# RWKV-7 attention and a cosine router: chunks of 64 steps instead of 32, two heads on the two row halves of TensorE

## The chip, the cores and the metric

The kernel runs on one core of a Trainium2 chip. The time is the device time of one execution in microseconds; the median of several runs counts. TensorE multiplies, VectorE, ScalarE and GpSimd work element by element, and SyncE (SP) issues most of the DMA transfers.

## What is computed

The first part is a recurrence over 768 steps for 4 batch elements and 8 heads, with a 40x40 state for each. Its output, as rows of 320 features for 3072 tokens, goes through a router with 8 experts, of which each token takes one; the expert is two matrix products with a ReLU between them.

```python
for t in range(S):
    y[:, :, t] = np.einsum('bhd,bhde->bhe', rt, state)
    Sa = np.einsum('bhde,bhe->bhd', state, at)
    state_decay = state * wt[:, :, None, :] - np.einsum('bhd,bhe->bhde', Sa, bt)
    state = state_decay + np.einsum('bhd,bhe->bhde', vt, kt)
...
logits = xn @ en.T / tau
expert_idx = np.argmax(logits, axis=1)
...
    h = np.maximum(x[mask] @ w1[e], 0.0)
    out[mask] = gate_w[mask, None] * (h @ w2[e])
```

## The kernel before

All arithmetic is in float32. The steps are cut into tiles of 128 (6 for each of 4 batch elements, 24 in all, `groups`), and a tile into 4 chunks of 32 steps. Features (40) or steps (128) stand on the partitions. Each tile goes through two generators.

`prepare` does what doesn't need the state: two scans over the decay w (L202, L205), scaling of a, k and b, transposes of the scaled inputs (`ln`, `an`, `kn`, `bn`, L237), four products between all 128 steps and all 128 steps of a tile for each head (`between`, L248: `ne`, `ge`, `fe`, and later `he`), of which a mask keeps the four 32x32 blocks on the diagonal (L251). Then it inverts the 32x32 triangular blocks in five levels: the first from a mask alone, then four times `w_ps` (L300), a copy on ScalarE, `x_ps` (L310), a predicated copy on VectorE (L314). These products are 32x32, and the four chunks stand on the diagonal of the array. Last come `te` (the inverse spread out to 128x128), `gv` and `pt`.

`advance` takes the state through the four chunks: `u_ps` (L359) against the state, `s_ps` (L367, L372) for the next state, `sn` (the state transposed, L384), `y_ps` against it (L388). At the end of a tile come `ut`, `he`, the rest of y, and the router: `xr`, its transposes `xt_ps`, the logits `lg_ps` (L418), some fifteen small steps on VectorE and ScalarE, and the store to `x_rows`.

While `advance` runs on a tile, two steps of `prepare` of the next are taken for each of its own, and a scheduler puts the instructions of every engine into one order from the dependencies and its own estimates. The buffers set when loads can start: most inputs have one buffer, some two. The eight parts of the expert weights `w2` are loaded one after the other in the attention (`load_w2`, L91, on ScalarE's queue) into memory of their own. `w1` is loaded when the attention has ended (L472 on SP, L475 on ScalarE), into memory that the attention used.

The experts run in 31 blocks of 128 tokens: gather, transposes (L607), `h_ps` (L628), transposes (L645), `y_ps` (L655), scatter. Which expert a block takes is a number in a register, and `h_ps` and `y_ps` index the whole of w1 and w2 with it, so the first `h_ps` waits for all of w1 and the first `y_ps` for all of w2.

A product in float32 is two instructions (passes) on TensorE, each with a load of its weights and a matmul; a transpose is one. In the trace, "xN" counts these.

Of the kernel before, what the change touches and what calls it, by code (L numbers as in the profile page):

```python
# [9 lines left out]
FP32 = mybir.dt.float32  # L10
BF16 = mybir.dt.bfloat16
I32 = mybir.dt.int32
# [8 lines left out]
L = 32  # L21
NCK = P // L

# [6 lines left out]
def kernel(  # L30
# [26 lines left out]

    nc = tc.nc
# [7 lines left out]
    CH = H * NCK  # L66
# [3 lines left out]
    XBUF = 3  # L70

# [6 lines left out]
    w2_sb = persist.tile([P, E, FC, DM], FP32, name="w2_sb")  # L78
    w2f = w2_sb.rearrange("p e c d -> p (e c d)")
# [10 lines left out]
    def load_w2(e):  # L90
        nc.scalar.dma_start(  # L91
            out=w2_sb[:, e], in_=moe_w2[e].rearrange("(c p) d -> p c d", p=P)
        )

    with ExitStack() as attn:
# [3 lines left out]
        mmp = attn.enter_context(tc.tile_pool(name="mmp", bufs=5, space=PSUM))  # L99
# [6 lines left out]
        blk = cst.tile([P, P], FP32, name="blk")  # L106
        nc.vector.memset(blk, 0.0)
        for c in range(NCK):
            nc.vector.memset(blk[L * c : L * c + L, L * c : L * c + L], 1.0)
        upper = cst.tile([P, P], FP32, name="upper")  # L110
        nc.gpsimd.affine_select(
            out=upper, in_=blk, compare_op=ALU.is_gt, fill=0.0, base=0,
            pattern=[[1, P]], channel_multiplier=-1,
        )
        nlower = cst.tile([P, P], FP32, name="nlower")
        nc.gpsimd.affine_select(
            out=nlower, in_=blk, compare_op=ALU.is_gt, fill=0.0, base=0,
            pattern=[[-1, P]], channel_multiplier=1,
        )
        nc.vector.tensor_scalar(nlower, nlower, -1.0, None, ALU.mult)  # L120
        icomp = cst.tile([P, L], FP32, name="icomp")
        nc.vector.tensor_reduce(
            icomp.unsqueeze(2), ident.rearrange("p (c j) -> p j c", c=NCK), axis=AX.X, op=ALU.add
        )
        rowi = cst.tile([P, L], I32, name="rowi")
        coli = cst.tile([P, L], I32, name="coli")
        nc.gpsimd.iota(rowi, pattern=[[0, L]], base=0, channel_multiplier=1)
        nc.gpsimd.iota(coli, pattern=[[1, L]], base=0, channel_multiplier=0)
        nc.vector.tensor_scalar(rowi, rowi, L - 1, None, ALU.bitwise_and)
        rowf = cst.tile([P, L], FP32, name="rowf")  # L130
        colf = cst.tile([P, L], FP32, name="colf")
# [5 lines left out]
        for j in range(L.bit_length() - 1):  # L137
            m = cst.tile([P, L], I32, name=f"level{j}")
# [6 lines left out]
        W1C = CH * (L + 1) + 1  # L145
        first = cst.tile([D, W1C], FP32, name="first")
        nc.vector.memset(first, 0.0)
        nc.vector.memset(first[:, 0 :: L + 1], 1.0)
        decay = cst.tile([D, W1C], FP32, name="decay")
        nc.vector.memset(decay[:, 0 :: L + 1], 0.0)  # L150


        emb = two.tile([P, XW], FP32, tag="xr", name="emb")[0:E, 0:DM]
# [3 lines left out]
        emb2 = two.tile([P, XW], FP32, tag="xr", name="emb2")[0:E, 0:DM]  # L157
# [13 lines left out]
        def h3(t):  # L171
            return t[:, 0:DM].rearrange("p (h d) -> p h d", h=H)

        def half(t):
            return t.rearrange("p (h x) -> p h x", h=4)

        state = {}
        groups = [(b, i) for i in range(NT) for b in range(B)]
        loaded = {}

        def load(g):
            b, i = groups[g]
            d = {}
            for nm, src in (("w", wT), ("a", aT), ("k", kT), ("b", bT), ("v", vT), ("r", rT)):
                t = (two if nm == "r" else one).tile([D, H, P], FP32, tag=f"in_{nm}", name=f"in_{nm}")
                nc.sync.dma_start(out=t, in_=src[b, i])
                d[nm] = t
            d["vn"] = two.tile([P, H, D], FP32, tag="vn", name="vn")
            nc.sync.dma_start(out=d["vn"], in_=v[b, i])
            loaded[g] = d  # L190

        def prepare(g, d):

            d.update(loaded.pop(g))
            ck = "p (x t) -> p x t"


            body = decay[:, 0 : W1C - 1].rearrange(ck, t=L + 1)
            nc.scalar.copy(body[:, :, 1:], d["w"].rearrange("p h (c t) -> p (h c) t", t=L))
            lam = one.tile([D, W1C], FP32, tag="lam", name="lam")  # L200
            suf = one.tile([D, W1C], FP32, tag="suf", name="suf")
            nc.vector.tensor_tensor_scan(  # L202
                lam, decay, first, initial=0.0, op0=ALU.mult, op1=ALU.add
            )
            nc.vector.tensor_tensor_scan(  # L205
                suf[:, ::-1], decay[:, ::-1], first[:, ::-1], initial=0.0, op0=ALU.mult, op1=ALU.add
            )
            lam3 = lam[:, 0 : W1C - 1].rearrange(ck, t=L + 1)
            lam_l = two.tile([D, CH], FP32, tag="lam_l", name="lam_l")
            nc.vector.tensor_copy(lam_l, lam3[:, :, L])  # L210
            d["lamL"] = lam_l.rearrange("p (h c) -> p h c", c=NCK)
            inv_l = two.tile([D, CH], FP32, tag="inv_l", name="inv_l")
            nc.vector.reciprocal(inv_l, lam_l)
            inv = d["w"].rearrange("p h (c t) -> p (h c) t", t=L)
            nc.gpsimd.tensor_tensor(
                inv,
                suf[:, 1:].rearrange(ck, t=L + 1)[:, :, 1:],
                bc(inv_l, [D, CH, L], 2),
                ALU.mult,
            )  # L220

            def chunked(t):
                return t.rearrange("p h (c t) -> p (h c) t", t=L)

            lx = one.tile([D, W1C], FP32, tag="suf", name="lx")[:, 0 : H * P].rearrange(
                "p (h t) -> p h t", h=H
            )
            nc.scalar.copy(chunked(lx), lam3[:, :, 0:L])
            nc.vector.tensor_tensor(d["a"], d["a"], lx, ALU.mult)
            nc.gpsimd.tensor_tensor(d["k"], d["k"], d["w"], ALU.mult)  # L230
            nc.gpsimd.tensor_tensor(d["b"], d["b"], d["w"], ALU.mult)


            for nm, src in (("ln", lx), ("an", d["a"]), ("kn", d["k"]), ("bn", d["b"])):
                ps = h3(bank(f"{nm}_ps"))
                for h in range(H):
                    nc.tensor.transpose(ps[:, h], src[:, h], ident[0:D, 0:D])  # L237
                d[nm] = (one if nm == "an" else two).tile([P, H, D], FP32, tag=nm, name=nm)
                nc.scalar.copy(d[nm], ps)
            yield  # L240

            def between(nm, lhs, rhs, mask, pool):
                t = pool.tile([P, H, P], FP32, tag=nm, name=nm)
                for q in range(2):
                    ps = half(bank(f"{nm}_ps"))
                    for j in range(4):
                        h = 4 * q + j
                        nc.tensor.matmul(  # L248
# [12 lines left out]
            if g + 1 < NG:  # L261
                load(g + 1)
# [464 lines left out]
```

## Time and profile before

| | us |
|---|---|
| median of 3 runs | 2146.05 (2144.84 to 2147.27) |
| profiled execution | 2144.23 |
| its span, first to last instruction | 2142.5 |
| TensorE busy | 2034.7 |
| VectorE, ScalarE, GpSimd busy | 692.4, 377.9, 298.1 |

In a row of the timeline stand the start, the time from there to the end of the last instruction of the group, the engine, the line, the operation, what it writes and reads (weights and moving operand), shapes, and the count. The difference of two starts is the time that a group holds the engine. The granted clock is a share of 2.4 GHz: 0.50 is the level of 1.2 GHz, 1.00 that of 2.4.

### The profile page before, as it was taken

Reading aid. Unit: us, or ns where it says so; the run is one execution under the profiler, and the core shown is the slowest. Engines: PE = TensorE matmul, PEld = TensorE weight load, DVE = VectorE, ACT = ScalarE, POOL = GpSimd, SP = SyncE. Lnnn points to the kernel's source line nnn. Section 1 sums busy time; section 2 is a strip of 40 time slices with the busy share of each in tenths; the row PEclk is TensorE's granted clock in tenths of the full one; section 3 lists DMA queues with packets and bytes.
Section 4 is the critical chain, followed back from the end, with each engine's and each line's share of the span. In section 5 each row is a group of like instructions: output and inputs, shape, how many; then the busy total and the mean of one; then the engine's idle time right before and its main releaser. Section 6 shows DMA issues by size and latency. Waiting matters only on the chain. (4 is left out here: it accounts for less than half of the span.)

```text
span 2142.5 us, 54098 instructions
## 1 busy us (share of the span) xinstructions
PE 2034.7 (95%) x24944; PEld 1725.1 (81%) x24944; DVE 692.4 (32%) x1374; ACT 377.9 (18%) x769; POOL 298.1 (14%) x240
## 2 busy tenths in 40 slices
PE   4999999999999999999999999999999948999998
PEld 4899989898989898989898988898898843555554
DVE  5332433243324332443234333432443231111111
ACT  1112112211211122112111211121211111111111
POOL 3011101110111011101110111011101011111110
PEclk9655555555555555555555555555555558999999
DMA  8000000000000000000000000000000042000000
GB/s 243 14 26 15 20 20 26 11 21 23 23 14 21 23 25 12 21 24 23 14 21 23 23 15 21 23 23 15 24 23 8 5 140 88 25 27 28 21 17 4
DMA packets 28481, 63.81 MB, mean 30 GB/s; under 512 B 4052, under 2 KB 18398, under 8 KB 28256
## 3 DMA queue, kind: packets, MB, share of 16 engines
q1 hardware_dynamic: 16320, 39.88, 6.3%
q10 hardware_dynamic: 8960, 12.58, 2.0%
q0 software_dynamic: 2976, 7.89, 1.2%
q8 instruction: 198, 3.24, 0.6%
q14 instruction: 27, 0.22, 0.0%
HBM read 53.60 MB, written 9.02 MB: 29 GB/s over the span
## 5 line engine op out<-in xcount | busy, mean ns | idle before, releaser
L628 PE MATMUL h_ps<-w_sb,xT 128*128 x372 | 185.5, 624 | 9.2 <-DMA w_sb<-in_moe_w_dram 9.2
L270 POOL TENSOR_TENSOR te<-xt,blk 128x1024 f32<-128x1024 f32 x24 | 56.4, 2349 | 976.1 <-DVE xt L314 976.1
L628 PEld LDWEIGHTS h_ps<-w_sb,xT 128*128 128x128 f32 x372 | 63.3, 190 | 115.6 <-issue 111.0
L655 PE MATMUL y_ps<-w_sb,hT 128*128 x496 | 138.8, 433 | 0.0
L388 PE MATMUL y_ps<-sn,in_r 40*32 40x40 f32 x1536 | 126.4, 265 | 6.8 <-ACT sn L386 6.8
L367 PE MATMUL s_ps<-vn,kn 32*40 32x40 f32 x1472 | 130.1, 265 | 0.0
L386 ACT COPY sn<-sn_ps 40x320 f32<-40x320 f32 x96 | 40.1, 418 | 506.0 <-PE sn_ps L384 506.0
L372 PE MATMUL s_ps<-un,bn 32*40 32x40 f32 x1472 | 126.1, 263 | 0.4 <-DVE gs L444 0.4
L359 PE MATMUL u_ps<-st,pt 40*32 40x40 f32 x1536 | 125.6, 264 | 0.0
L300 PE MATMUL w_ps<-xt,ne 32*32 32x32 f32 x6144 | 121.1, 238 | 3.9 <-DVE xt L314 3.9
L388 PEld LDWEIGHTS y_ps<-sn,in_r 40*32 40x32 f32 x1536 | 107.3, 162 | 20.9 <-ACT sn L386 10.0
L367 PEld LDWEIGHTS s_ps<-vn,kn 32*40 32x40 f32 x1472 | 108.2, 173 | 15.0 <-issue 5.4
L310 PE MATMUL x_ps<-ws,xn 32*32 32x32 f32 x6144 | 104.0, 237 | 16.5 <-ACT ws L305 12.9
L655 PEld LDWEIGHTS y_ps<-w_sb,hT 128*128 128x128 f32 x496 | 91.7, 190 | 34.2
L359 PEld LDWEIGHTS u_ps<-st,pt 40*32 40x32 f32 x1536 | 106.7, 162 | 14.5 <-issue 8.8
L300 PEld LDWEIGHTS w_ps<-xt,ne 32*32 32x32 f32 x6144 | 99.7, 149 | 18.6 <-DVE xt L314 4.3
L372 PEld LDWEIGHTS s_ps<-un,bn 32*40 32x40 f32 x1472 | 108.6, 174 | 7.4 <-DVE gs L444 0.5
L310 PEld LDWEIGHTS x_ps<-ws,xn 32*32 32x32 f32 x6144 | 90.9, 150 | 25.7 <-ACT ws L305 16.3
L251 DVE TENSOR_TENSOR he<-he_ps,upper 128x512 f32<-128x512 f32 x48 | 32.8, 684 | 230.1 <-PE he_ps L248 230.1
L305 ACT COPY ws<-w_ps 128x256 f32<-128x256 f32 x96 | 35.7, 372 | 362.5 <-PE w_ps L300 362.5
L248 PE MATMUL fe_ps<-in_r,in_v 40*128 40x128 f32 x384 | 98.4, 435 | 0.0
L322 PE MATMUL gv_ps<-vn,ge 128*128 128x40 f32 x384 | 92.3, 416 | 0.0
(179 smaller groups left out, 3172.7 us busy)
## 6 DMA issues: line engine op xcount, KB each, us to landing
w_sb<-in_moe_w_dram ACTq DMA_DIRECT2D x8, 1280.0 KB
w_sb<-in_moe_w_dram SPq DMA_DIRECT2D x8, 1024.0 KB
x_rows<-xr SPq DMA_DIRECT2D x24, 160.5 KB
in_w<-in_wT_dram SPq DMA_DIRECT2D x24, 160.0 KB
in_a<-in_aT_dram SPq DMA_DIRECT2D x24, 160.0 KB
in_k<-in_kT_dram SPq DMA_DIRECT2D x24, 160.0 KB
in_b<-in_bT_dram SPq DMA_DIRECT2D x24, 160.0 KB
in_v<-in_vT_dram SPq DMA_DIRECT2D x24, 160.0 KB
```

The source lines that it names most:

```text
L248: nc.tensor.matmul(ps[:, j], lhsT=lhs[:, h], rhs=rhs[:, h], start=True, stop=True)
L270: nc.gpsimd.tensor_tensor(t.rearrange("p h (c j) -> p h c j", c=NCK), bc(x, [P, H, NCK, L], 2), bc(blk.rearrange("p (c j) -> p c j", c=NCK ...
L300: nc.tensor.matmul(ps[rows, h], lhsT=ne[rows, h, rows], rhs=xt[rows, h], start=True, stop=True, skip_group_check=True,)
L310: nc.tensor.matmul(ps[rows, h], lhsT=xd[rows, h], rhs=ws[rows, h], start=True, stop=True, skip_group_check=True,)
L322: nc.tensor.matmul(gv_ps[:, h], lhsT=ge[:, h], rhs=d["vn"][:, h], start=True, stop=True)
L359: nc.tensor.matmul(u_ps[rows, h], lhsT=d["pt"][:, h, rows], rhs=st[:, h], start=False, stop=True, skip_group_check=True,)
L367: nc.tensor.matmul(s_ps[:, h], lhsT=d["kn"][rows, h], rhs=d["vn"][rows, h], start=(h == 0), stop=False, skip_group_check=True,)
L372: nc.tensor.matmul(s_ps[:, h], lhsT=d["bn"][rows, h], rhs=un[rows, h], start=False, stop=True, skip_group_check=True,)
L386: nc.scalar.copy(sn, sn_ps)
L388: nc.tensor.matmul(y_ps[rows, h], lhsT=d["r"][:, h, rows], rhs=sn[:, h], start=False, stop=False, skip_group_check=True,)
L628: nc.tensor.matmul(ps, lhsT=d["xT"][0:kn, c], rhs=w1f[0:kn, ds(ek * (len(KC) * F) + c * F + q * 512, 512)], start=(c == 0), stop=(c == len ...
L655: nc.tensor.matmul(ps, lhsT=d["hT"][:, c], rhs=w2f[:, ds(d["ek"] * (FC * DM) + c * DM, DM)], start=(c == 0), stop=(c == FC - 1),)
```

## The change

The attention is written anew; the experts are as before but for the loading of their weights.

- Two batch elements go together as one unit (12 units). A chunk is 64 steps long, so a tile has two. Of a pair of heads one has its 40 features on partitions 0 to 39, the other on 64 to 103; the index of such pairs is x (8 in a unit), of the head in a pair par. An input of a unit comes in four loads (w in sixteen); the partitions between are filled once at the start, on GpSimd.
- `gram` replaces `between`: only products within a chunk, 64x64, with par and chunk naming the part of the array. The inverse is still of 32x32 blocks, in four levels after the first (now from `nd`, small products of its own); the lower left 32x32 block of the inverse of a chunk comes from one more step (the half level and `z`).
- Products that write steps are cut into 32 columns of the array (`sub`): `gv`, u against the state (named u_ps at L422 in the order), u, y against `sn`, y, `lg`.
- `pt`, `an` and the product that spreads `te` are gone. `sn` is a product with an identity, no transpose, and the old state comes into `s_ps` by a product with the identity.
- Two steps of `prepare` are still taken for each of `advance`, and `kn`, `ge`, `bn`, `fe` stand between w and x of the four levels (`fill`). More inputs have two or three buffers.
- PSUM has seven rotating banks and one for s, before five and three.
- `w2` gets memory that the attention has used, and is loaded behind it with w1, w1 on SP and w2 on ScalarE.

```diff
-L = 32
+L = 64
+SB = 32
+NP = 4
+OFF = 64
...
-    w2_sb = persist.tile([P, E, FC, DM], FP32, name="w2_sb")
...
+        units = [(i, bp) for i in range(NT) for bp in range(BP)]
+        feat = [slice(0, D), slice(OFF, OFF + D)]
+        chunk = [slice(0, L), slice(L, P)]
+        sub = [slice(SB * q, SB * q + SB) for q in range(P // SB)]
...
+        def gram(nm, lhs, rhs):
+            ps = [bank(f"{nm}_ps").rearrange("p (x t) -> p x t", x=NX) for _ in range(2)]
+            for x in range(NX):
+                for c in range(2):
+                    for par in range(2):
+                        nc.tensor.matmul(
+                            ps[par][chunk[c], x], lhsT=lhs[feat[par], x, chunk[c]],
+                            rhs=rhs[feat[par], x, chunk[c]],
+                            start=True, stop=True, skip_group_check=True,
+                        )
+            return ps
...
+            for m_ in levels[1:]:
+                xd = turned(xt)
+                ps = blocks(
+                    "w_ps", lambda ps, m, q: mm(ps[sub[q], m], ne[sub[q], m, own(q)], xt[sub[q], m])
+                )
+                ws = two.tile([P, NM, SB], FP32, tag="ws", name="ws")
+                nc.scalar.copy(ws, ps)
+                yield
+                if fill:
+                    fill.pop(0)()
+                ps = blocks(
+                    "x_ps", lambda ps, m, q: mm(ps[sub[q], m], xd[sub[q], m], ws[sub[q], m])
+                )
+                nc.vector.copy_predicated(xt, bc(m_, [P, NM, SB], 1), ps)
+                yield
...
+            def with_state(ps, lhs, st, c):
+                for x in range(NX):
+                    for s_ in range(2):
+                        q = 2 * c + s_
+                        for par in range(2):
+                            mm(ps[par][sub[q], x], lhs[feat[par], x, sub[q]], st[feat[par], x, 0:D])
...
+                    for x in range(NX):
+                        for par in range(2):
+                            mm(s_ps[feat[par], x], kn[rows, 2 * x + par], vn[rows, 2 * x + par], False)
...
+                                mm(
+                                    u_ps[bb][sub[2 * c + s_], p, par],
+                                    d["te"][rows, mi(x, par), SB * s_ : SB * s_ + SB],
+                                    ru[rows, x, par],
+                                )
...
-            if g % 2 == 1 and g // 2 < E:
-                load_w2(g // 2)
...
+    w2_sb = wpool.tile([P, E, FC, DM], FP32, name="w2_sb")
...
-        nc.scalar.dma_start(out=w1_sb[0 : KC[2][1], e, 2], in_=moe_w1[e, 2 * P : DM])
+        nc.sync.dma_start(out=w1_sb[0 : KC[2][1], e, 2], in_=moe_w1[e, 2 * P : DM])
+        nc.scalar.dma_start(
+            out=w2_sb[:, e], in_=moe_w2[e].rearrange("(c p) d -> p c d", p=P)
+        )
```

On TensorE, in the middle of a tile, the order of before puts the two products of a level (w_ps, x_ps, for 8 heads) between the state's products for a chunk of 32 steps:

```order
L310 MATMUL x_ps<-ws,xn 32x32 x32
L359 MATMUL u_ps<-st_2247,pt 32x40 x8
L367 MATMUL s_ps<-vn,kn 40x40 x6
L300 MATMUL w_ps<-xt,ne 32x32 x32
L367 MATMUL s_ps<-vn,kn 40x40 x2
L372 MATMUL s_ps<-un,bn 40x40 x4
L310 MATMUL x_ps<-ws,xn 32x32 x32
```

and the changed kernel, at the same place, for 16 heads and a chunk of 64:

```order
L348 MATMUL w_ps<-xt,ne 32x32 x64
L301 MATMUL kn_ps<-ident,in_k_150 128x104 x8
L348 MATMUL x_ps<-ws,xn 32x32 x64
L422 MATMUL s_ps<-un_172,bn 40x40 x16
L492 MATMUL ut_ps<-ident,un_172 104x64 x8
L348 MATMUL w_ps<-xt,ne 32x32 x64
L241 MATMUL ge_ps<-in_a_144,in_k_150 64x64 x32
L348 MATMUL x_ps<-ws,xn 32x32 x64
```

The products that stood behind the levels (kn, ge, bn, fe) now stand between w and x of one level, and the state's products between two levels. On TensorE at the end of a tile and into the next, before:

```order
L331 MATMUL pt_ps<-te,an 40x128 x7
L347 MATMUL y_ps<-kn,fe 128x40 x2
L237 MATMUL ln_ps<-ident,lx 128x40 x8
L237 MATMUL an_ps<-ident,in_a 128x40 x8
L237 MATMUL kn_ps<-ident,in_k 128x40 x8
L237 MATMUL bn_ps<-ident,in_b 128x40 x8
L248 MATMUL ne_ps<-in_b,in_a 128x128 x4
```

and in the changed kernel at the end of a unit:

```order
L422 MATMUL y_ps<-kn,fe 32x40 x64
L422 MATMUL y_ps<-bn,he 32x40 x64
L530 MATMUL xt_ps<-ident,xr 128x128 x2
L530 MATMUL xt_ps<-ident,xr 64x128
L422 MATMUL s_ps<-st_0_176,ident 104x320
L541 MATMUL lg_ps<-embT,xs 32x8 x8
```

There pt, an and the whole-array products are gone, and y is made of 32-column pieces right ahead of the router's transposes.

## Rows read from the trace of the kernel before

**Rows 1.** The page: busy time, share and instructions by engine; granted clock in 40 slices.
```profile
PE 2034.7 (95%) x24944; PEld 1725.1 (81%) x24944; DVE 692.4 (32%) x1374; ACT 377.9 (18%) x769; POOL 298.1 (14%) x240
...
PEclk9655555555555555555555555555555558999999
```

**Rows 2.** TensorE timeline: one place in two tiles, the last tile.
```profile
643.70 1.17 PE L248 MATMUL ne_ps<-in_b,in_a 40*128 40x128 f32 x8
...
1640.72 1.47 PE L248 MATMUL ne_ps<-in_b,in_a 40*128 40x128 f32 x8
...
1706.64 0.25 PE L384 MATMUL sn_ps<-ident,st 40*40 40x40 f32 x2
...
1735.71 1.55 PE L418 MATMUL lg_ps<-embT,xs 128*128 128x8 f32 x6 [0.46 <-ACT xs L414]
```

**Rows 3.** TensorE timeline of the tile from 606 us on: one group of each kind.
```profile
606.10 1.27 PE L359 MATMUL u_ps<-st,pt 40*32 40x40 f32 x16
607.30 0.75 PE L367 MATMUL s_ps<-vn,kn 32*40 32x40 f32 x8
607.98 1.08 PE L310 MATMUL x_ps<-ws,xn 32*32 32x32 f32 x64
...
612.89 0.72 PE L384 MATMUL sn_ps<-ident,st 40*40 40x40 f32 x8
613.54 3.21 PE L322 MATMUL gv_ps<-vn,ge 128*128 128x40 f32 x14
...
618.33 1.91 PE L397 MATMUL ut_ps<-ident,un 128*40 128x128 f32 x8
...
642.70 0.67 PE L237 MATMUL kn_ps<-ident,in_k 40*128 40x40 f32 x8
...
647.07 3.62 PE L248 MATMUL ge_ps<-in_a,in_k 40*128 40x128 f32 x16
```

**Rows 4.** Groups by line and shape: busy us, mean ns, idle before.
```profile
L300 PE MATMUL w_ps<-xt,ne 32*32 32x32 f32 x6144 | 121.1, 238 | 3.9 <-DVE xt L314 3.9
...
L202 DVE TENSOR_TENSOR_SCAN lam<-decay,first 40x1057 f32<-40x1057 f32 x24 | 55.5, 2314 | 6.6 <-ACT decay L199 6.6
...
L305 ACT COPY ws<-w_ps 128x256 f32<-128x256 f32 x96 | 35.7, 372 | 362.5 <-PE w_ps L300 362.5
L229 DVE TENSOR_TENSOR in_a<-in_a,lx 40x1024 f32<-40x1024 f32 x24 | 33.4, 1392 | 3.1 <-ACT lx L228 3.1
...
L251 DVE TENSOR_TENSOR he<-he_ps,upper 128x512 f32<-128x512 f32 x48 | 32.8, 684 | 230.1 <-PE he_ps L248 230.1
```

**Rows 5.** TensorE timeline: first gram, and first transposes of the second tile.
```profile
26.07 3.76 PE L248 MATMUL ne_ps<-in_b,in_a 40*128 40x128 f32 x16
...
69.58 0.69 PE L237 MATMUL ln_ps<-ident,lx 40*128 40x40 f32 x8
```

**Rows 6.** VectorE timeline: a fill at the start.
```profile
1.27 0.94 DVE L147 MEMSET first<- 40x1057 f32 x1 [0.16 <-issue]
```

**Rows 7.** Chain that ended last: start us, us, what.
```profile
1743.00 19.50 DMA w_sb<-in_moe_w_dram
```

**Rows 8.** TensorE timeline: first products of the experts.
```profile
1779.73 8.40 PE L628 MATMUL h_ps<-w_sb,xT 128*128 x12 [9.18 <-DMA w_sb<-in_moe_w_dram]
...
1795.33 0.70 PE L655 MATMUL y_ps<-w_sb,hT 128*128 x2
```

**Rows 9.** Window, TensorE: its length, busy (count), granted clock, DMA share, GB/s.
```profile
47.50:50.00 2.50, 0.00 (x0) 1.00 1.07 373
```

**Rows 10.** Windows, TensorE, same columns, around the end of a tile.
```profile
642.00:644.00 2.00, 2.00 (x32) 1.00 0.00 0
...
646.00:648.00 2.00, 2.00 (x11) 0.50 0.00 0
```

**Rows 11.** TensorE timeline: a pt group, and s_ps at the upper clock.
```profile
637.87 3.21 PE L331 MATMUL pt_ps<-te,an 128*40 128x128 f32 x14
...
1708.51 0.80 PE L372 MATMUL s_ps<-un,bn 32*40 32x40 f32 x16 [0.39 <-DVE gs L444]
```

More of the change, by code (lines that the diff above doesn't have):

```diff
@@ L103, in bank @@
             return mmp.tile([P, 512], FP32, tag="mm", name=name)
[L106 to L110, printed above, removed]
+        id2 = cst.tile([P, L], FP32, name="id2")
+        nc.vector.tensor_tensor(id2, ident[:, 0:L], ident[:, L:P], ALU.add)
+        upper = cst.tile([P, L], FP32, name="upper")
+        wide = cst.tile([P, P], FP32, name="wide")
@@ L111 @@
+        nc.vector.memset(wide, 1.0)
         nc.gpsimd.affine_select(
-            out=upper, in_=blk, compare_op=ALU.is_gt, fill=0.0, base=0,
+            out=wide, in_=wide, compare_op=ALU.is_gt, fill=0.0, base=0,
             pattern=[[1, P]], channel_multiplier=-1,
         )
[L115 to L119, printed above, removed]
@@ L192, in prepare @@
[L192 to L201, printed above, removed]
+        units = [(i, bp) for i in range(NT) for bp in range(BP)]
+        NU = len(units)
+        feat = [slice(0, D), slice(OFF, OFF + D)]
@@ new lines, in masked, with mi, prepare @@
+        def masked(nm, ps, pool):
+            t = pool.tile([P, NM, L], FP32, tag=nm, name=nm)
+            for par in range(2):
+                nc.vector.tensor_tensor(
+                    t[:, NX * par : NX * par + NX], ps[par], bc(upper, [P, NX, L], 1), ALU.mult
+                )
+            return t
+        def mi(x, par):
+            return NX * par + x
+        def prepare(u, d):
+            d.update(loaded.pop(u))
+            seg = "p (g t) -> p g t"
+            decay = d["decay"]
+            lam = one.tile([FP, W1C], FP32, tag="lam", name="lam")
+            suf = one.tile([FP, W1C], FP32, tag="suf", name="suf")
@@ L207, in prepare @@
             )
[L208 to L214, printed above, removed]
+            inv_l = two.tile([FP, SEG], FP32, tag="inv_l", name="inv_l")
@@ L234, in prepare @@
[L234 to L248, printed above, removed]
-                            ps[:, j], lhsT=lhs[:, h], rhs=rhs[:, h], start=True, stop=True
-                        )
-                    nc.vector.tensor_tensor(
-                        t[:, 4 * q : 4 * q + 4], ps, bc(mask, [P, 4, P], 1), ALU.mult
-                    )
-                return t
@@ L292, in prepare @@
-            nc.vector.copy_predicated(xt, bc(levels[0], [P, H, L], 1), turned(nn))
-            yield
-            for m in levels[1:]:
-                xd = turned(xt)
-                ps = c3(bank("w_ps"))
-                for h in range(H):
-                    for c in range(NCK):
-                        rows = slice(L * c, L * c + L)
+            ps = gram("ne", d["a"], d["b"])
+            ne = one.tile([P, NM, L], FP32, tag="ne", name="ne")
+            for par in range(2):
+                nc.scalar.copy(ne[:, NX * par : NX * par + NX], ps[par])
@@ new lines, in mm, with own @@
+            def mm(o, lhsT, rhs):
+                nc.tensor.matmul(o, lhsT=lhsT, rhs=rhs, start=True, stop=True, skip_group_check=True)
+            def own(q):
+                return slice(SB * (q % 2), SB * (q % 2) + SB)
+            fill = [
+                lambda: d.update(kn=natural("kn", lambda x: d["k"][:, x], 1.0)),
+                lambda: d.update(ge=masked("ge", gram("ge", d["k"], d["a"]), one)),
+                lambda: d.update(bn=natural("bn", lambda x: d["b"][:, x], 1.0)),
+                lambda: d.update(fe=masked("fe", gram("fe", d["v"], d["r"]), two)),
+            ]
@@ L456 @@
             pass
-        for g in range(NG):
+        for u in range(NU):
             now, ready = ready, {}
-            ahead = prepare(g + 1, ready) if g + 1 < NG else iter(())
-            for _ in advance(g, now):
+            ahead = prepare(u + 1, ready) if u + 1 < NU else iter(())
+            for _ in advance(u, now):
                 next(ahead, None)
```

521 lines of the change are left out of this document (300 added, 221 removed).

## The prediction

> **What bounds the kernel now.** I read the shares first: TensorE is busy for 95% of the span, VectorE for 32%, and no other engine for more than 18% [rows 1]. The clock line of the same group shows that the attention, up to the 32nd of forty slices, runs at about half clock and the experts at nearly full clock. Next I took the period of a tile. In the TensorE timeline the first half of ne stands at 643.70 and again at 1640.72, fourteen tiles later [rows 2], so a tile takes 997.0/14 = 71.2 us and two tiles 142.4. The last tile, which has no next one to prepare, goes from 1706.64 to its router product lg at 1735.71. The rest, 1735.71 to the end of the span at 2142.5, is 406.8 us: the end of the router, the loading of w1, and 31 blocks of the experts.
>
> Is the 142.4 all TensorE work? I priced each kind of product by the rows of its group, an fp32 product being two passes and a transpose one [rows 3]. u_ps: 1.27 us for 16 passes, 79 ns; so for s_ps and y_ps against the state. x_ps and w_ps, four 32x32 tiles on the diagonal of the array: 1.08/64 = 16.9 ns. Products of 128x128 on 40 rows (ge and its like): 3.62/16 = 226. Those with 128 weight columns and 40 moving (gv and its like): 3.21/14 = 229. Transposes: ut 1.91/8 = 239, sn 0.72/8 = 90, ln to bn 0.67/8 = 84; xt about 0.30, lg 1.55/6 = 0.26. Two tiles have 128 passes of the 226 kind (28.9 us), 160 of the 229 kind (36.6), 1024 at 16.9 (17.3), 512 at 79 (40.4), 64 sn (5.8), 16 ut (3.8), 64 short transposes (5.4), 6 xt (1.8) and 12 lg (3.1): 143.1 us. So the period is the sum of TensorE's passes, with nothing left for waits, and group prices, which contain the end of each group, hold the switches between groups as well.
>
> **The change part by part.** *Rate of a pass.* The new products stand on quarters or eighths of the array, and successive ones on different parts. The only place where the trace shows this is x_ps: a pass every 16.9 ns, where one N=40 pass alone takes 79, or 63 if scaled to 32 columns (an estimate from the u_ps row). So four tiles that differ in rows and columns run together, 3.7 times as fast as one. I use 79/4 = 20 ns for 32-column products on four tiles, and half the price of ge, 113, over four, 28 ns, for 64x64. Products that share their rows and differ only in columns (u, and both s products) appear nowhere alone; bounds are one and two at a time, 79 and 39.5 ns. I take 39.5, since the row that is nearest, x_ps, shows no loss from company.
>
> Here a rule speaks against me. In u_ps all 16 passes stand on one row group, and one follows each 79 ns; its 40 moving columns cost all of that, so the next weights were loaded under it. The Trainium skill (TensorE: Matmul & The Clock Gate, Part 3) says that a weight load overlaps matmuls in flight only where the row group differs. By that rule tiles with the same rows would gain nothing, and the sum would be the rows-only rival below; u_ps disagrees at least for loads.
>
> *One unit (two batch elements, so two old tiles).* 24 transposes with 104 moving columns, 239x104/128 = 194 ns: 4.7 us. 16 ut at half of 239: 1.9. Four grams, 256 passes at 28.3: 7.2. nd, 128 at 16.9: 2.2. Four levels, 1024 at 16.9: 17.3. The half level, 64 passes on two tiles, 34 ns: 2.2. z: 2.2. gv, u against the state, y against sn, and y: 640 passes at 19.7: 12.6. u and the two s: 256 at 39.5: 10.1. sn, now a product with 64 weight columns on two tiles, 229/4 = 57: 64 passes, 3.7. The state through the identity, 4 passes of 320 columns, 8x79: 2.5. lg 48 at 16.9: 0.8. xt 1.8. Sum **69.2 us** against 142.4. Gone are pt, an, the te product and the wide halves of the masked products that were zeros.
>
> *Do the others follow?* Each VectorE instruction now does two tiles at once. Scans on 104 partitions have the price of those on 40, 2.31 us; masks 0.68 each; copies of 512 columns stand near it [rows 4]. With two scans, six masks, ten turns and predicated copies of about 0.7, one 1.4 us multiply and some thirty small ones VectorE has about 27 us of work a unit; ScalarE, at 0.37 us for 256 columns, about 18. In the order each w or x group is separated from the next of its chain by 1 to 4 us of other products, more than the 0.6 to 0.8 us of copy between them. The end of a unit (masked he, xr, xt, lg) waits some 1 to 2 us; TensorE has the same pause before (part of the 142.4), so I add nothing. Cover is gone if passes get much faster (clock rival).
>
> *Start.* ne starts at 26.07 and the first tile is ready at 69.58 [rows 5]. Now 20 padding fills stand on GpSimd; at the 0.94 us of a fill of 1057 columns on VectorE [rows 6] the one of decay is done about 15 us in, the second half of w lands behind it at about 20, and the chain behind it (two scans of 2.3, the copy lx, multiplies on GpSimd and VectorE, some 10 us) puts ne at 30. Alone, a unit then needs about 5 us to the first w, four levels of about 7 (two groups of 2.2, copies 1.4, the fill), and 7 for the rest: 68. Range 60 to 80.
>
> *Last unit.* Two chunks in a chain of about 7.5 us, then ut, he, y, xr, xt, lg: 28 against 29.1.
>
> *Expert weights.* w2 is no longer loaded under the attention. Before, w1 (10.5 MB) moves from 1743.00 and h_ps, which can index any expert and so waits for all, starts at 1779.73: 36.7 us, 286 GB/s [rows 7]; the first y_ps follows at 1795.33 [rows 8]. Now 21 MB move there in two queues, and y_ps waits for all of w2. At 286 to 373 GB/s (the window 47.5 to 50, w2 and inputs together [rows 9]) that is 56 to 73 us. If w1 is done first, y_ps starts at 56 instead of 52.3, +4; if both end together at 73, h_ps starts then and y_ps at 89, +37. I take **+22**, the middle.
>
> **Sum.** 68 + 11x69.2 + 28 + 406.8 + 22 = 1286.0 us of span; the profiled execution took 2144.23 with a span of 2142.5, so 1.7 more: 1287.7 against 2144.23, 856 us less. The median is 2146.05, 1.8 above it, so I say **1288**.
>
> **The rivals.**
> *Clock.* Before, after each pt group (128 rows, 128 moving columns, 637.87) the granted clock goes to 1.00 for a few us, and the 40-row products that follow bring it back to 0.50 [rows 10, 11]. At the upper level s_ps takes 0.80 us for 16, 50 ns instead of 79 [rows 11]. The new gv, z and y, some 10 us in a row on all 128 rows, resemble pt, which speaks for it; that x_ps, on 128 rows too, has a granted clock of 0.50 before and after it speaks against. All of a unit at 0.63 is 44 us, with waits now open about 52: 65 + 11x52 + 26 + 406.8 + 22 + 1.7 = 1093; half of it, 61 a unit, 1194.
> *Rows only.* Tiles with equal rows take turns. Grams 14.5, nd 4.3, the 640 passes 25.3, u and s 20.2, lg 3.2: 34.6 us more, 103.8 a unit: 70 + 1141.8 + 36 + 406.8 + 22 + 1.7 = 1678. For it: no row of before shows two column tiles on the same rows. Against: the u_ps row.
> *Drain between shapes.* A unit has about 45 changes of tile shape. If each emptied the array, at the 238 ns that a w_ps pass lasts from its start to its end [rows 4], that would be 10.7 us a unit, 1416 in all. Against: x_ps at 607.98 starts 0.68 us after 8 passes of s_ps did [rows 3], and 8x79 is 0.63: 0.05 us is left for the change. The Trainium skill (TensorEngine Tiling (Array Packing), Key Properties) says that a change of tiling mode drains TensorE; the trace shows 0.05 us, so at most a short one.
> *One at a time (slower).* If half-array tiles don't run together at all, grams cost 28.9, nd 8.7, the 640 passes 50.6, u and s 20.2, sn 7.4, lg 3.2: 151.6 a unit, 80 + 1667.6 + 48 + 430.5 = 2226. It decides from 144 us a unit on, (2144.2 - 430.5 - 80 - 48)/11; so nearly all of the concurrency would have to be missing.
>
> **How the numbers follow.** Forecast 0.46, with a range of its own from 1200 to 1370; clock 0.22; drain 0.11; rows only 0.14; one at a time 0.05; other 0.02. From 1080 to 1500 the range holds the forecast, the clock case and the drain, and leaves out rows only and one at a time, 0.19. A measurement of this kernel can tell 0.2% from no change. Faster 0.95, same 0.01, slower 0.04.
>
> **What would show it.** Right: w_ps of two units lie 65 to 74 us apart, TensorE is busy over 90% between, 16 u_ps passes take 0.6 us and a gram 1.8; granted clock near 0.5 in the attention; h_ps or y_ps waits for the weights, y_ps 56 to 89 us behind their start. A gram of 3.6 us is rows only, one of 7 one at a time. A granted clock of 0.7 or more and gaps ahead of w_ps and x_ps are the clock case. It would be wrong if VectorE stood in the chain between two levels, or if loads, now 38 a unit on SP, held up lam.

## The result, and the profile after

| | before | after |
|---|---|---|
| median, us | 2145.45 (4 runs) | 1438.82 (1436.12 to 1446.72, 4 runs) |
| ratio | 1 | 0.6714, interval 0.6691 to 0.6738 |
| profiled execution and its span | 2144.23, 2142.5 | 1446.72, 1444.9 |

The time lies in the predicted range of 1080 to 1500, 151 us above the point of 1288, and above 1200 to 1370, the range of the forecast itself without its rivals. The page of the changed kernel, with the rows that answer to [rows 1], the rows on instruction transfers, and the instruction row of the kernel before, which was not shown:

```profile
span 1444.9 us, 69656 instructions
...
PE 1141.3 (79%) x33004; PEld 881.9 (61%) x33004; DVE 407.7 (28%) x814; ACT 271.8 (19%) x541; POOL 234.9 (16%) x223
...
PEclk9965555556555555556555555655559999999999
...
q8 instruction: 261, 4.28, 1.2%
q14 instruction: 22, 0.18, 0.0%
```

```profile
q8 instruction: 198, 3.24, 0.6%
```

TensorE is no longer busy for 95% of the span but for 79%, and no other engine has come near to it. So something else takes time, and it is not the arithmetic of VectorE.

The TensorE timeline gives the period, as in [rows 2]: the transposes kn of a unit stand at

```profile
101.41 1.65 PE L301 MATMUL kn_ps<-ident,in_k 104*128 104x104 f32 x8
...
915.05 1.65 PE L301 MATMUL kn_ps<-ident,in_k 104*128 104x104 f32 x8
```

Ten units take 813.64 us, 81.4 each, against 69.2 predicted. The window over just these ten units (columns as in [rows 9]) and the waits of TensorE in it (us in total, times, longest) say where the difference is:

```profile
101.41:915.05 813.64, 649.34 (x26583) 0.55 0.12 33
```

```profile
PE y_ps L422 <- issue: 34.1, 27, 2.2
PE w_ps L348 <- issue: 30.2, 24, 1.8
PE u_ps L422 <- issue: 29.8, 18, 2.7
PE x_ps L348 <- issue: 23.9, 32, 1.8
...
PE xt_ps L530 <- POOL xr L520: 2.8, 6, 0.5
```

TensorE works for 64.9 us in a unit, less than the 69.2 that were priced, and idles for 16.4. All rows with "issue" sum to 158.6 us, 15.9 a unit: time in which TensorE waits for nothing that the profile shows. Waits for VectorE, GpSimd and ScalarE together are under half a microsecond a unit. Before, the same view of fourteen tiles, 643.70 to 1640.72, has no "issue" row at all.

In the timeline these stalls have a rhythm. A stretch in the sixth unit:

```profile
533.80 1.49 PE L348 MATMUL x_ps<-ws,xn 32*32 32x32 f32 x91
535.70 0.75 PE L348 MATMUL x_ps<-ws,xn 32*32 32x32 f32 x37 [0.42 <-issue]
...
539.73 0.88 PE L422 MATMUL y_ps<-sn,in_r 40*32 40x40 f32 x37 [0.54 <-issue]
540.54 1.48 PE L348 MATMUL w_ps<-xt,ne 32*32 32x32 f32 x90
543.79 0.76 PE L348 MATMUL w_ps<-xt,ne 32*32 32x32 f32 x38 [1.77 <-issue]
...
547.66 1.60 PE L348 MATMUL x_ps<-ws,xn 32*32 32x32 f32 x103 [0.69 <-issue]
```

Work resumes at 535.70, 539.73, 543.79 and 547.66: 4.03, 4.06 and 3.87 us apart, and between two stalls stand about 128 passes (from 539.73: 37 of y, 90 of w). A stall falls in the middle of a product group, whose operands have long been there. A pass is two instructions, so 128 are 256 instructions. The page gives the size of one: 4.28 + 0.18 MB of instruction transfers over 69656 instructions is 64 bytes, and 4.28 MB over 261 packets is 16.4 KB, 256 instructions a packet. The Trainium skill (Perfetto Trace Analysis, The 4-stage abstract model) gives 64 bytes too. The DMA rows of the ten units count the blocks themselves (packets, MB, share of the time of 16 DMA engines):

```profile
q8 instruction: 208, 3.41, 1.8%
```

That is one packet for 128 of the 26583 passes, every 3.91 us. The reading to be tested: instructions come to TensorE in blocks of 256, and a block takes some 3.9 us to come, whatever is in it. In the middle of the attention of before this could not show: the 1986 passes that the prediction priced for two tiles took 142.4 us, 9.2 us for 128.

The rates of the passes are near those of the prediction. A gram stands at 824.57 with 64 passes, and the next product follows 1.91 us later:

```profile
824.57 1.99 PE L241 MATMUL ne_ps<-in_b,in_a 40*64 40x64 f32 x64
826.48 0.77 PE L322 MATMUL nd_ps<-in_a,in_b 40*32 40x32 f32 x52
```

The end, to be read against [rows 2, 7, 8]: the router's product, then the first products of the experts, and the first DMA of the chain of waits:

```profile
1003.41 0.56 PE L541 MATMUL lg_ps<-embT,xs 128*32 128x8 f32 x24 [0.46 <-ACT xs L534]
...
1079.94 10.59 PE L751 MATMUL h_ps<-w_sb,xT 128*128 x12 [38.96 <-DMA w_sb<-in_moe_w_dram]
...
1097.71 0.70 PE L778 MATMUL y_ps<-w_sb,hT 128*128 x2
```

```profile
1011.30 40.04 DMA w_sb<-in_moe_w_dram
```

From lg to the end of the span are 441.5 us, against 406.8 before.

### The profile page after: what moved, and what is told of

Its sections match the earlier page's. It is cut to its first block, busy times and chain, and to the rows that moved or that the text cites. A ratio compares the mean times of both kernels' runs of the same rounds, so it can differ in the third digit from the quotient of the medians.

```text
span 1444.9 us, 69656 instructions
## 1 busy us (share of the span) xinstructions
PE 1141.3 (79%) x33004; PEld 881.9 (61%) x33004; DVE 407.7 (28%) x814; ACT 271.8 (19%) x541; POOL 234.9 (16%) x223
## 3 DMA queue, kind: packets, MB, share of 16 engines
q8 instruction: 261, 4.28, 1.2%
## 5 line engine op out<-in xcount | busy, mean ns | idle before, releaser
L348 PE MATMUL x_ps<-ws,xn 32*32 32x32 f32 x6144 | 101.2, 232 | 28.6 <-issue 28.3
L372 DVE COPY_PREDICATED xt<-level,x_ps 128x512 f32<-128x512 int32 x48 | 35.0, 730 | 234.7 <-PE x_ps L348 234.7
L758 ACT ACTIVATE h<-h_ps 128x512 f32<-128x512 f32 x62 | 37.1, 598 | 222.8 <-PE h_ps L751 222.8
L784 POOL DMA_INDIRECT out_dram<-y,prm x31 | 31.4, 1012 | 224.0 <-DVE gt L732 174.7
L422 PE MATMUL u_ps<-ru,te 64*32 64x40 f32 x1536 | 51.0, 243 | 19.7 <-issue 19.7
L422 PEld LDWEIGHTS u_ps<-ru,te 64*32 64x32 f32 x1536 | 46.0, 146 | 21.9 <-issue 21.2
L715 POOL DMA_INDIRECT xin<-x_rows,prm x31 | 31.8, 1027 | 125.9 <-PE xt_ps L730 125.2
L422 PE MATMUL sn_ps<-id,st 40*64 40x40 f32 x768 | 44.7, 296 | 1.2 <-issue 1.1
L422 PE MATMUL u_ps<-st,in_a 40*32 40x40 f32 x1536 | 35.8, 258 | 12.1 <-issue 12.1
L279 DVE TENSOR_TENSOR_SCAN suf<-decay,first 104x1041 f32<-104x1041 f32 x12 | 45.3, 3777 | 0.0
L422 PE MATMUL y_ps<-bn,he 64*32 64x40 f32 x1536 | 31.9, 265 | 15.4 <-issue 15.3
```

Source lines behind the costliest of these rows:

```text
L279: nc.vector.tensor_tensor_scan(suf[:, ::-1], decay[:, ::-1], first[:, ::-1], initial=0.0, op0=ALU.mult, op1=ALU.add)
L348: nc.tensor.matmul(o, lhsT=lhsT, rhs=rhs, start=True, stop=True, skip_group_check=True)
L372: nc.vector.copy_predicated(xt, bc(m_, [P, NM, SB], 1), ps)
L422: nc.tensor.matmul(o, lhsT=lhsT, rhs=rhs, start=start, stop=True, skip_group_check=True)
L715: nc.gpsimd.indirect_dma_start(out=xins[j % XBUF], out_offset=None, in_=x_rows[:], in_offset=bass.IndirectOffsetOnAxis(ap=prm[:, j : j + 1 ...
L758: nc.scalar.activation(h[:, 512 * q : 512 * q + 512], ps, AF.Relu)
```

## The experiments

The theory is *supply*: each block of 256 instructions costs TensorE the longer of its execution and some 3.5 to 4 us. Its rivals are that TensorE's own work sets the period (then an added or removed pass counts in full), that waits for other engines or loads make the gaps, and the prediction's rows-only case. "Period" is the mean over ten units between two kn groups, for e8 over the first eight of them. The kernels after, e4, e6 and e8 ran four times each, the others once, so that a difference of some 10 us, as of e3, says nothing by itself.

| kernel | us | period | TensorE busy in it | passes in the kernel |
|---|---|---|---|---|
| after | 1438.8 | 81.4 | 64.9 | 33004 |
| e1_extra | 1517.7 | 88.1 | 78.4 | 33196 |
| e2_two_levels | 1280.2 | 68.1 | 57.0 | 26860 |
| e3_rows_only | 1452.4 | 81.3 | 71.4 | 33004 |
| e4_wide | 1391.9 | 76.8 | 67.8 | 29164 |
| e5_w1_first | 1418.4 | | | |
| e6_wide_w1 | 1377.7 | 77.1 | 69.0 | 29164 |
| e8_levels | 1451.0 | 84.0 | 82.9 | 23020 |

**More work in few instructions (e1_extra).** Eight products more in a unit:

```diff
+            def extra():
+                nc.tensor.matmul(
+                    bank("extra"), lhsT=d["v"][feat[0], 0], rhs=d["r"][feat[0], 0:4],
+                    start=True, stop=True, skip_group_check=True,
+                )
...
+                extra()
                 ws = two.tile([P, NM, SB], FP32, tag="ws", name="ws")
...
+                extra()
                 nc.vector.copy_predicated(xt, bc(m_, [P, NM, SB], 1), ps)
```

> Behind each w and each x group of the four levels stands one more product that nothing reads: 40 rows, 128 columns, 512 moving columns, two passes of about 0.86 us at the half clock (four times the 0.22 us of a pass with 128 moving columns). That is 8 a unit, 13.8 us of TensorE time and only 32 instructions. Theory of supply (TensorE waits for its instructions, a block of 256 each 3.9 us): the extra time falls mostly into the 15.9 us a unit in which TensorE has nothing to issue, and the kernel takes 1450 to 1500 us. Rival (TensorE's own work or waits for data set the period): 12 times 13.8 us more, about 1600 us.

TensorE works 13.5 us more in a unit, and the period grows by 6.7. Half of the added work costs nothing; the stalls had room for it. That is between the two theories' values, 18 us above the upper end for supply, so neither expectation holds as it stands. The expectation had taken the stalls of a unit as one store. The likely reason, read from the waits and not tested by a run of its own, is that an addition, here 1.7 us at each of eight places, fills only the block in which it stands, and the other blocks go on stalling: from 101 to 915 us some 89 us of "issue" are left.

**Less of both (e2_two_levels).** Two of the four levels are left out, so the inverse is incomplete; the fill that stood in them follows behind.

```diff
-            for m_ in levels[1:]:
+            for m_ in levels[1:3]:
...
```

> Two of the four levels are left out, so the inverse is not complete. That takes 512 passes, 1024 instructions or four blocks, and 8.0 us of TensorE time (15.7 ns each) out of a unit. Theory of supply: four blocks of 3.9 us less, 13 to 15.7 us a unit, 1250 to 1285 us. Rival (TensorE's work sets the period): 8.0 us a unit, about 1342 us; and if it were the waits between levels, anything between.

A unit has 512 passes less. TensorE's work falls by 7.9 us a unit, the period by 13.3: more goes than was worked. Four blocks of 3.92 would be 15.7; part of that is used up by a new wait, 24.1 us in ten units in which y waits for the masked he. By TensorE's work alone 12 x 7.9 = 95 us would have gone, and 159 went.

**The order that should take turns (e3_rows_only).** The products are the same, in an order in which successive passes keep their 32 or 64 columns of the array and change the rows, as for gram:

```diff
-            for x in range(NX):
-                for c in range(2):
+            for c in range(2):
+                for x in range(NX):
                     for par in range(2):
...
```

> Only the order of the products within a group is changed: successive passes keep to the same columns of the array as long as they can, so that at most the two row halves can run together (u and both s products one at a time). Theory that tiles with the same rows and other columns run together when they follow each other: TensorE's work rises by the 34.6 us a unit of the prediction's rows-only case to about 100 us, the supply of instructions no longer sets the period, about 1660 us. Rival (order doesn't matter, or columns never ran together): 1439 us as now.

1452.4 is near the value for an order that changes nothing, but not for that reason. In the TensorE timeline of this kernel one gram at the lower and one at the upper clock, and the windows that give the clock for them:

```profile
515.80 3.47 PE L241 MATMUL ge_ps<-in_a,in_k 40*64 40x64 f32 x64
...
556.82 1.91 PE L241 MATMUL he_ps<-in_r,ut 40*64 40x64 f32 x64
```

```profile
516.00:519.00 3.00, 3.00 (x64) 0.50 0.00 0
557.00:558.50 1.50, 1.50 (x62) 1.00 0.08 18
```

At the granted clock of 0.50 the gram takes 54 ns a pass instead of 30, as if half as many tiles ran together: the order does matter. But TensorE's work grew by 6.5 us a unit and the period not at all, because the longer passes lie in what would have been stalls: the "issue" rows of its ten units sum to 90.4 us, 6.8 a unit less. Its granted clock is 0.68 over these units instead of 0.55. By the theory the clock rival would have brought little, since a faster pass waits for its block; no run changes the clock alone.

**Fewer instructions, more work (e4_wide).** The products that write steps get 64 columns of weights instead of twice 32, as y:

```diff
-                        for s_ in range(2):
-                            for c in range(2):
-                                mm(
-                                    y_ps[bb][sub[2 * c + s_], h],
-                                    mat[chunk[c], m, SB * s_ : SB * s_ + SB],
-                                    nat[chunk[c], bb, h],
-                                    mat is d["fe"] and h == 0,
-                                )
+                        for c in range(2):
+                            mm(
+                                y_ps[bb][chunk[c], h], mat[chunk[c], m], nat[chunk[c], bb, h],
+                                mat is d["fe"] and h == 0,
+                            )
```

and in the same way gv, u and y against the state; 640 passes of a unit become 320.

> gv, u against the state, y against sn, and y are made of 64-column pieces, two tiles at a time, instead of 32-column pieces, four at a time. 640 passes become 320, 640 instructions or 2.5 blocks less a unit; TensorE's work rises from 640 at 20 ns (12.6 us) to 320 at 57 ns (18.2 us), 5.6 us a unit. Theory of supply: 7 to 9.8 us a unit less, 1320 to 1365 us, although TensorE has more to do. Rival (TensorE's work sets the period): 5.6 us a unit more, about 1505 us.

The ratio to before is 0.6475 (0.6459 to 0.6491). TensorE works 2.9 us a unit more and the period is 4.6 shorter, which a TensorE that was bound by its work could not do. The gain is 47 us and not the 74 to 119 of the expectation, whose upper end counts each of the 320 passes saved at a full 31 ns, a block's 3.92 us over 128. The largest of the stalls that are left, from 101.4 to 915 us, sit at the levels:

```profile
PE x_ps L348 <- issue: 21.7, 26, 2.0
PE w_ps L348 <- issue: 19.3, 22, 1.8
```

**The supply by itself (e7_probe).** Between attention and experts, on operands that are long there and with the DMA all but quiet:

```diff
...
+        ways = (
+            lambda j: (j % 4, j % 4),
+            lambda j: (0, 0),
+            lambda j: (0, j % 4),
+            lambda j: (j % 4, 0),
+        )
+        for k, way in enumerate(ways):
+            ps = [bank(f"p{k}_ps").rearrange("p (m t) -> p m t", m=NM) for _ in range(4)]
+            for j in range(512):
+                ro, co = way(j)
+                nc.tensor.matmul(
+                    ps[ro][sub[co], (j // 4) % NM], lhsT=pa[sub[ro], 0:SB], rhs=pb[sub[ro], 0:SB],
+                    start=True, stop=True, skip_group_check=True,
+                )
```

> Between the attention and the experts 2048 additional products of 32x32 with 32 moving columns (4096 passes) stand in four groups of 1024 passes: on the four tiles of the diagonal of the array; all on one tile; on four column tiles of the same rows; on four row tiles of the same columns. Nothing waits inside a group and no load runs. If the supply of instructions limits, a block of 256 instructions (128 passes) takes the longer of its execution and some 3.5 to 4 us: the diagonal takes about 31 us (30 ns a pass) though x_ps runs at 16 within a block, one tile about 65 us (63 ns) and shows no such gaps. Rival, that the gaps in the attention come from its waits or its loads: the diagonal takes 16 us. If tiles with the same rows run together, the third group takes as long as the first, if they take turns 65 us; the fourth likewise for the same columns. In all some 130 to 200 us more than 1438.8.

The TensorE timeline of this stretch, and windows in the first and second group (length, busy and count, granted clock, DMA share, GB/s):

```profile
991.76 3.21 PE L600 MATMUL p_ps<-pb,pa 32*32 32x32 f32 x222 [2.23 <-DVE pb L589]
...
1011.61 1.93 PE L600 MATMUL p_ps<-pb,pa 32*32 32x32 f32 x128 [1.55 <-issue]
1015.10 1.93 PE L600 MATMUL p_ps<-pb,pa 32*32 32x32 f32 x128 [1.56 <-issue]
1018.59 58.23 PE L600 MATMUL p_ps<-pb,pa 32*32 32x32 f32 x1280 [1.56 <-issue]
1078.43 1.93 PE L600 MATMUL p_ps<-pb,pa 32*32 32x32 f32 x128 [1.61 <-issue]
...
1111.94 1.93 PE L600 MATMUL p_ps<-pb,pa 32*32 32x32 f32 x128 [2.10 <-issue]
```

```profile
1010.00:1020.00 10.00, 5.33 (x313) 0.50 0.02 5
1040.00:1045.00 5.00, 5.00 (x98) 0.50 0.01 3
```

This is the supply alone. Blocks of exactly 128 passes start 3.49 us apart, sometimes 3.75 or 4.03; 1.93 us of that is work, 15.1 ns a pass with the end of the last one counted in, and the rest is "issue", with no semaphore, no load and no other engine in play. The second group, all on one tile, has no gap: 98 passes in 5 us are 51 ns each (the expectation had 63), 6.5 us a block, which is longer than the block takes to come. The third and the fourth group (1078.43 is in the third, 1111.94 in the fourth) run exactly like the first: four column tiles on the same rows, or four row tiles on the same columns, run together as well as four on the diagonal. The slow group doesn't build up a store either: behind the 222 and six blocks of 128, the row of 1280 passes holds the last 34 of the first group, the 1024 of the second and 222 of the third, so that after some 54 us of slow passes the rest of one block and one block more came without a gap, and then the stalls begin again. The rival without a limit gave 16 us for the first group; it took 27 (991.76 to 1019.1), its first blocks having come ahead. In all the kernel takes 1562.3: from lg at 988.97 to the end are 571.5 us, 130 more than in the changed kernel, with an attention that ended 14 us sooner in this execution.

**The weights (e9_late_w2, e5_w1_first, e6_wide_w1).** e9 is the kernel before with w2 loaded as in the changed one, and nothing else:

```diff
-            if g % 2 == 1 and g // 2 < E:
-                load_w2(g // 2)
...
-        nc.scalar.dma_start(out=w1_sb[0 : KC[2][1], e, 2], in_=moe_w1[e, 2 * P : DM])
+        nc.sync.dma_start(out=w1_sb[0 : KC[2][1], e, 2], in_=moe_w1[e, 2 * P : DM])
+        nc.scalar.dma_start(
+            out=w2_sb[:, e], in_=moe_w2[e].rearrange("(c p) d -> p c d", p=P)
+        )
```

> The kernel before with one part of the change alone: w2 is loaded behind the attention with w1, as in the changed kernel. If the weights' term there is this loading alone, h_ps starts some 70 us behind the start of the loads and y_ps some 88 instead of 52, so +35 us: about 2180. If the longer boundary of the changed kernel has another cause, the two stay apart: 2150 to 2168 (the prediction's +4 to +22).

2176.35, 29.9 above the median of before in the same comparison: from lg at 1737.56 to the end are 437.1 us, 30.3 more than before. So this edit alone accounts for 30 of the 35 us that the changed kernel's end is longer. Its h_ps waits for all of w1, which now shares the transfer with w2:

```profile
1812.37 7.89 PE L624 MATMUL h_ps<-w_sb,xT 128*128 x12 [42.99 <-DMA w_sb<-in_moe_w_dram]
```

The order of the loads can give part of that back:

```diff
-        nc.sync.dma_start(out=w1_sb[0 : KC[2][1], e, 2], in_=moe_w1[e, 2 * P : DM])
-        nc.scalar.dma_start(
+        nc.scalar.dma_start(out=w1_sb[0 : KC[2][1], e, 2], in_=moe_w1[e, 2 * P : DM])
+    for e in range(E):
+        (nc.sync if e % 2 == 0 else nc.scalar).dma_start(
             out=w2_sb[:, e], in_=moe_w2[e].rearrange("(c p) d -> p c d", p=P)
         )
```

> The changed kernel with w1 on both queues first and w2 behind it. If h_ps waits because w1 shares the transfer with w2, h_ps starts about 37 to 42 us behind the start of the loads instead of 70, and y_ps then waits for w2 at about 70 instead of 88: about 1420. Rival, that the amount of both together sets h_ps: no change, 1438.

In its timeline, with the loads issued from 1003.08 on:

```profile
1044.68 10.21 PE L752 MATMUL h_ps<-w_sb,xT 128*128 x12 [12.65 <-DMA w_sb<-in_moe_w_dram]
...
1069.13 6.90 PE L779 MATMUL y_ps<-w_sb,hT 128*128 x16 [4.72 <-DMA w_sb<-in_moe_w_dram]
```

h_ps starts 41.6 us behind the start of the loads, y_ps 66.1, and from lg to the end are 420.1 us, 21.4 less. Together with e4:

> Both edits that help by the theory: the 64-column products and w1 first. They stand in different stages, so the gains add: 1392 - 18 = about 1374. If the loading is hidden anyway: 1392.

1377.71, ratio 0.6423 (0.6402 to 0.6445): 61 us less than the changed kernel, of 47 and 20 that the two gave alone. It is the fastest of these kernels that leave nothing out.

**Still fewer instructions (e8_levels).** On top of e6, in the four levels, one 64x64 weight tile with zeros off the diagonal in place of two of 32x32:

```diff
...
-                xd = turned(xt)
-                ps = blocks(
-                    "w_ps", lambda ps, m, q: mm(ps[sub[q], m], ne[sub[q], m, own(q)], xt[sub[q], m])
+                xd = spread(turned(xt))
+                ps = halves(
+                    "w_ps", lambda ps, m, c: mm(ps[chunk[c], m], bd[chunk[c], m], xt[chunk[c], m])
                 )
...
```

> On top of 64-column products and w1 first, the products of the four levels take two 32x32 blocks at a time as one 64x64 weight tile with zeros off the diagonal: 64 passes a group instead of 128, 512 passes (1024 instructions) a unit less. On TensorE a pass of 64x64 with 32 moving columns on two tiles takes about 31 ns (63/2) against 16, so a group takes 2.0 us as before and TensorE's busy time stays. VectorE has the same, ScalarE and GpSimd each some 3 us a unit more. By the supply of instructions the 9 us of issue stalls that are left in a unit go for the most part: 1374 - 60 to 90 = 1285 to 1315. Rival, that these stalls are dependencies of the levels, or that the added steps stand in the chain: 1374 or more.

It is slower, 1451.0, and yet its waits agree with the theory. All waits of TensorE of any size in eight units, a group of w at 519 us, and one of x at 801 us:

```profile
PE nd_ps L327 <- issue: 3.0, 3, 1.2
PE u_ps L437 <- issue: 3.0, 3, 1.3
PE y_ps L437 <- issue: 1.8, 4, 0.8
PE z_ps L369 <- issue: 0.6, 2, 0.4
PE y_ps L437 <- DVE he L256: 0.5, 2, 0.3
```

```profile
519.06 3.68 PE L369 MATMUL w_ps<-xt,bd 64*64 64x32 f32 x63
522.67 1.65 PE L306 MATMUL kn_ps<-ident,in_k 104*128 104x104 f32 x8
...
801.06 3.63 PE L369 MATMUL x_ps<-ws,xw 64*64 64x32 f32 x64
```

The stalls are gone, 8.4 us in eight units, where the changed kernel has 15.9 in each. But the edit does two things at once, fewer instructions and slower passes: 14610 passes in eight units are 14.3 blocks a unit, each with 5.8 us of work, longer than it takes to come. So e8 alone doesn't tell which of the two ended the stalls. A pass takes 57 ns (3.61 us for 63) and not the 31 that I expected from the moving columns: what sets it fits the 64 columns of weights. Two tiles together at 57 ns would make 114 for one alone (an estimate), twice the 51 of one tile with 32 weight columns in e7, with the same 32 moving columns; a gram, with 64 weight and 64 moving columns, comes to 120 by the same estimate, four tiles at 30. TensorE's work grows by 13.9 us a unit over e6, most of it here, and only 8.1 of idle time were there to take. The Trainium skill (TensorE: Matmul & The Clock Gate, Part 2, Step-by-step) says that the time of a weight load goes by its columns and not by its rows; these rows agree as far as they go, since the gram has 40 rows and the products of e8 64.

## Why the prediction was right, and where it was off

By its own terms, for the profiled execution:

| term | predicted | measured |
|---|---|---|
| start, to the first u_ps | 68 | 82.4 |
| eleven units, to the first u_ps of the last, 975.78 | 11 x 69.2 = 761.2 | 893.3, 81.2 each |
| last unit, to lg | 28 | 27.6 |
| from lg to the end | 428.8 | 441.5 |
| span | 1286.0 | 1444.9 |

- *What bounded the kernel before* and the direction were right: the sum of TensorE's passes, with hardly a wait in it. The prediction's "nothing left for waits" is a little strong: the waits of fourteen tiles sum to 19.8 us, 2.8 for two tiles, which the group prices had taken in.
- *The rate of a pass* was right: 64.9 us of work in a unit against 69.2. A gram takes 30 ns a pass (28.3 predicted), 32x32 passes 15.1 in e7 (16.9), u 32 to 33 and s 38 to 40 in the changed kernel (39.5, the lower of the two bounds).
- *The step that failed* is the one from this sum to the period. I compared 69.2 with 142.4, added nothing for waits, and looked for what would be late next only among VectorE, ScalarE, copies and loads. None of these came late; the instructions did. The 15.9 us of issue stalls and half a microsecond of other waits, less the 4.3 by which the work was over-priced, make the 12 us a unit, 132 in all. A warning stood in the trace: the instruction row of the page gives the size of a block, and 1024 passes of 17 ns are 256 instructions in 2.2 us, where the kernel before takes 9.2 us for as many on average. And the limit itself shows once before the change, in the first tile, where the levels run with no other products between them:

```profile
50.35 0.54 PE L310 MATMUL x_ps<-ws,xn 32*32 32x32 f32 x22 [3.07 <-issue]
51.45 1.08 PE L300 MATMUL w_ps<-xt,ne 32*32 32x32 f32 x64 [0.55 <-DVE xt L314]
53.07 0.79 PE L310 MATMUL x_ps<-ws,xn 32*32 32x32 f32 x41 [0.55 <-ACT ws L305]
54.48 0.54 PE L310 MATMUL x_ps<-ws,xn 32*32 32x32 f32 x23 [0.61 <-issue]
```

Two stalls fall inside an x group, 4.13 us apart, with 127 passes between them: the rhythm of the changed kernel. Neither the prediction nor the rows ahead of it have these. That the stalls follow the instructions is shown by e7, where nothing else is in play, and by e4, where fewer instructions with more work take less time; e2, e3 and e8 agree.
- *The start* was 14.4 us too short. lam waits for w until 23.98, ne starts at 33.83 (30 predicted), and then the levels stall for instructions as well, as at 47.22 with 1.62 us and 69.52 with 1.29 before it, 7.9 us in all up to the first u_ps. It was read from the trace only; no kernel here takes it apart.
- *The weights* cost 35 us and not 22, near the upper bound of 37, and e9 gives 30 for the loading alone. The mechanism was that of the upper bound: w1 ends late because it shares the transfer, at 69.9 us behind its issue (73 in the prediction's "both end together"). y_ps then waits for h and not for w2. Taking the middle of two cases with one mechanism each was the mistake; e5, with 420.1 us from lg to the end, 13.3 more than before, shows that even to come near the lower case (+4) takes another order of the loads.
- *The rivals.* Rows only is refuted by e7's third group: tiles on the same rows run at 15.1 ns, like those on the diagonal. The rule weighed against u_ps (the Trainium skill, TensorE: Matmul & The Clock Gate, Part 3: a weight load overlaps only where the row group differs) would leave that group no load under a matmul of the same rows, so that it should be slower than the diagonal, and it is not. One at a time falls with it. The drain has nothing left to explain, since TensorE's work, changes of shape included, is below the sum priced without one. The clock case didn't come: the granted clock stayed at a mean of 0.55. The prediction's own signs say the same: a gram takes 1.9 us and y_ps starts 87.6 us behind the start of the loads, as foreseen, but the period is 81.4 and not 65 to 74, and TensorE is busy for 80% of it and not over 90%.

The time came out above the drain case, 1416, and below rows only, 1678, for a reason that was none of the named ones. That the range up to 1500 held it is luck as to the mechanism: it was drawn that wide for the drain, which didn't come.

## What to carry to other kernels

Cutting a product into pieces that run side by side makes each pass cheap, but not its instructions: count each 256 instructions (128 passes, a weight load and a matmul each) at no less than the 3.5 to 4 us that a block took here, and compare that with the execution time of the same block, before believing a sum of passes. Rows with "issue" in the middle of a product group, about 128 passes apart, are its mark; then merging pieces helps even where TensorE works longer (e4), up to the point where the weight columns cost more than the stall (e8). And loads that move out of the cover of other work should be ordered by who waits for them first.

## What the runs showed that I had not expected

- Instructions reach TensorE at about 16.4 KB in 3.5 to 4 us, some 4 to 4.7 GB/s, with the DMA nearly idle (share 0.01 to 0.03 in e7). From 1078 to 1124 us of e7 13 packets took 1.8% of 16 engines' time, about 1.0 us each, so the transfer itself is under a third of it; what fills the rest isn't shown, nor why a block takes 3.49 once and 4.03 another time. The input loads can lengthen a block only a little in the changed kernel: in its last of the ten units, 835.69 to 915.05, the DMA moved 8 GB/s instead of 33, and the unit took 79.4 us against the mean of 81.4. In the first tile of before, with 358 GB/s from 48 to 50 us, the stall was the longest seen, 3.07 us; no run tests whether the load is the cause.
- Four 32x32 tiles give a pass every 15.1 ns at the granted clock of 0.50 for all three ways to place them, against 51 for one.
- In e8 the granted clock reads 1.00 up to about 600 us and 0.50 behind it, yet w takes 57 ns a pass at 519 us and x the same at 801. In e3 the same record goes with a gram's time. So it can't be read alone; why it doesn't fit in e8 stays open:

```profile
519.00:522.00 3.00, 3.00 (x64) 1.00 0.03 5
...
760.00:915.00 155.00, 153.21 (x3534) 0.53 0.07 20
```
